# Moving one of eight convolution groups from the middle of a fused kernel to behind its last table

## The chip, the core and the metric

The kernel runs on one core of a Trainium2 chip. The metric is the device time of one execution in microseconds (us); the median of three runs is given. The core has five engines, each with its own instruction queue: TensorE (PE, matrix products, with its weight loads listed as PEld), VectorE (DVE), ScalarE (ACT), GpSimd (POOL) and SyncE (SP, which mostly issues DMA transfers). They wait for each other through semaphores. PE writes to PSUM, and DVE or ACT must carry the result from there to SBUF ("evacuation").

## What is computed

Two long convolutions over 2048 steps and 448 channels share one input x, and a gate mixes them. Branch A builds its convolution kernel K from a table of complex powers; branch B multiplies a shifted k with v first and has its kernel given as data (`ssm_k`).

```python
g = sigmoid((x * gate_w).sum(-1))
# A: state space convolution, K[d, l] = Re sum_n C dB exp(dt A l)
P = exp(logdA[:, :, None] * l)            # the power table, 448 x 256 x 2048
K = einsum("dn,dnl,dn->dl", Cc, P, dB).real
a = causal_conv(u=x, K) + x * Dskip
# B: gated convolution
kv = shift_conv4(k, shift_k) * v
b = x * (causal_conv(kv, ssm_k) + kv * ssm_D)
return g * a + (1 - g) * b                # bf16, 1 x 2048 x 448
```

The reference does both causal convolutions by FFT. The kernel does them with matrix products: a two-stage transform of the signal and of the convolution kernel, a product, and a two-stage way back.

## The kernel before

The channels are cut into four groups of 4 x 28 (`NC = 28`), for each branch: groups ("A", 0..3) and ("B", 0..3). The convolution kernels of A are made by eight table blocks, `block(0)` to `block(7)`, two for each A group. A block is a run of DVE multiplications and additions (the power table in factors TQ and TP), 224 small matmuls that sum over the modes into `pk`, an evacuation of the sums, a gather, and a spread:

```python
def block(self, j, evac, behind=None):      # KGen
    ...                                     # DVE: TQ and TP, in one chain of order
    self.last = chain[0]                    # the last DVE operation of this table
    with self.tc.high_priority(offset=100000):
        ...                                 # PE: 14 x 2 x 2 x 4 matmuls into pk
        self.summed = evac(S[:], pt.rearrange("p n b -> p b n"))   # ACT
    return S
```

A convolution group goes through these helpers. `evac` is a copy on ACT.

```python
def spread_in(cols):                        # first half of the transform: 56 matmuls, 4 evacuations
    zs = qt([P, 32, 4 * NC], "zs")
    spread(nc, psum, Wc, zs, cols, ...)
    return zs

def transform(nc, psum, W, zs, evac, ...):  # second half: 32 matmuls, 4 evacuations
    ...

def swapped(zs, op=None):                   # a copy with its halves exchanged, by two DMAs
    swap = qt([P, 32, 4 * NC], "zsS")
    for r in range(2):
        d = nc.sync.dma_start(swap[64 * r:64 * r + 64], zs[64 - 64 * r:128 - 64 * r])
        ...                                 # behind op, the evacuation of a table's sums
    return zs, swap

def products(nc, X, S, Y, k0=0, k1=32):     # two DVE multiplications of 128 x 3584
    fl = lambda t: t[:, k0:k1].rearrange("p k c -> p (k c)")
    for t in (S, X):
        nc.vector.tensor_tensor(out=fl(t), in0=fl(t), in1=fl(Y), op=ALU.mult)
    return X, S

def stage_a(nc, psum, pool, R, terms, evac):      # way back, first stage: 56 matmuls, 4 evacuations to U
    ...
def stage_b(nc, psum, G, U, consume, banks=2):    # second stage: 128 matmuls, consume per half
    ...
def epilogue_B(H):                                # ug = conv * ug on DVE, from PSUM, twice a group
    ...
```

The loop over the groups consumes one group (`c`), prepares the next (`n`), and builds one table in each step:

```python
def step(c, n, j):
    kind, H = n
    if kind == "B":
        KB[H] = spread_in(skc.pop(H))
        XB[H] = spread_in(kv_cols(H))
    else:
        XA[H] = spread_in(u_cols(H))
    with tc.high_priority(offset=300000):
        U = stage_a(nc, psum, qp, R, terms[c], evac)
    if kind == "B":
        transform(nc, psum, W2, KB[H], evac)
        transform(nc, psum, W2, XB[H], evac)
    else:
        transform(nc, psum, W2, XA[H], evac)
    with tc.high_priority(offset=200000):
        stage_b(nc, psum, G, U, (hold_y if c == ("A", NQG - 2) else epilogue_A if c[0] == "A" else epilogue_B)(c[1]))
    ...
    block(j)
    if kind == "B":
        with tc.high_priority(offset=200000):
            terms[n] = products(nc, *swapped(KB[H], kg.summed), XB[H])
    else:
        XA[H] = swapped(XA[H], kg.summed)
    if kind == "A" and H < NQG - 1:
        transform(nc, psum, W2, KA[H], evac)
        with tc.high_priority(offset=200000):
            terms[n] = products(nc, *XA[H], KA[H])

seq = [("B", 0), ("B", 1), ("B", 2), ("A", 0), ("B", 3), ("A", 1), ("A", 2), ("A", 3)]
for j in range(NBLK - 1):
    step(seq[j], seq[j + 1], j)

# the tail: the last table and the last A group, in two halves
U = qt([P, 2, 64, NC], "U")
...
transform_half(nc, psum, W2, KA[3], evac, 0)
last(0)                                     # products of the first half
block(NBLK - 1)                             # the last table
transform_half(nc, psum, W2, KA[3], evac_two, 1)
stage_a_half(nc, psum, U, R, XA[3], evac, 0)
last(1)
mix_y(NQG - 2)
stage_a_half(nc, psum, U, R, XA[3], evac, 1)
stage_b(nc, psum, G, U, epilogue_A(3), 1)   # stores the output as it goes
```

The large tiles (`zs`, `zsS`, `zsK`, `U`, and the two pairs of `kv` blocks) share a pool of 8 buffers (`NBQ`); PSUM work shares 3 buffers. The order of instructions on each engine isn't that of the program text: a scheduler builds it from the dependencies, the priorities (`high_priority` with a larger offset goes first) and a time model, when the kernel is built.

Of the kernel before, what the change touches and what calls it, by code (L numbers as in the profile page):

```python
# [10 lines left out]
ALU = mybir.AluOpType  # L11
# [6 lines left out]
P = 128  # L18
# [4 lines left out]
NQG = 4  # L23
NC = 112 // NQG
CB = NC // 2
NBLK = 2 * NQG
# [25 lines left out]
def after(tc, ins, before):  # L52
    tc.add_manual_dep(ins.ins, before.ins.name,
                      mybir.DependencyInfo(mybir.DependencyClass.NoSync, mybir.DependencyReason.DATA),
                      reason="order on one engine")
# [6 lines left out]
class Consts:  # L62
# [67 lines left out]
    def stage_a(self, s_col, off_col):  # L130
        nc = self.nc
        j = self.iota("sa_j", [[1024, 64]])
        ph = self.carve(256).rearrange("p (i b) -> p i b", i=4)
        for i, off in enumerate((off_col[0][:, 0:1], off_col[1][:, 0:1], HALF, QUARTER)):
            self.phases(ph[:, i, :], j, s_col, off)
        R = self.pool.tile([P, 256], bf16, name="sa_R")
        nc.scalar.activation(R[:], low16(ph.rearrange("p i b -> p (i b)")), ACT.Sin, scale=PHASE)
        return R

    def stage_b(self, pool, qt, hqt, k_col, mask):  # L140
        nc = self.nc
        G = pool.tile([P, 64, 2, 4, 32], bf16, name="sb_G")
        jv = self.iota("sb_j", [[8, 16], [512, 32]]).rearrange("p (b a) -> p b a", b=16)
        offs = self.pool.tile([P, 4, 2], f32, name="sb_offs")
        for b0 in range(0, 64, 16):
            ph = qt([P, 16, 2, 32], "sb_ph", i32)
            for r, turn in enumerate((QUARTER, HALF)):
                o = offs[:, b0 // 16, r:r + 1]
                nc.vector.tensor_scalar(out=o, in0=k_col[:], scalar1=8.0 * b0, scalar2=turn, op0=ALU.mult, op1=ALU.add)
                self.phases(ph[:, :, r, :], jv, k_col, o)  # L150
            v = pool.tile([P, 16, 2, 32], bf16, name="sb_v", tag="kg_P4", bufs=2)
            nc.scalar.activation(v[:].rearrange("p b r a -> p (b r a)"), low16(ph[:].rearrange("p b r a -> p (b r a)")),
                                 ACT.Sin, scale=PHASE)
            for g in range(4):
                nc.vector.tensor_scalar(out=G[:, b0:b0 + 16, :, g, :], in0=v[:], scalar1=mask[:, g:g + 1], scalar2=None, op0=ALU.mult)
        return G
# [64 lines left out]
def transform(nc, psum, W, zs, evac, ks=range(4)):  # L221
    n = 4 * NC
    for kk in ks:
        pt = psum.tile([P, 2, 512], f32, name="ps_2", tag="ps")
        for i in range(8):
            k = 8 * kk + i
            nc.tensor.matmul(pt[:, i // 4, (i % 4) * n:(i % 4 + 1) * n], lhsT=W[:, k].rearrange("p r s -> p (r s)"), rhs=zs[:, k],  # L227
                             start=True, stop=True)
        evac(zs[:, 8 * kk:8 * kk + 8].rearrange("p (i k) c -> p i (k c)", i=2), pt[:, :, 0:4 * n], kk % 2)
# [6 lines left out]
def transform_half(nc, psum, W, zs, evac, half):  # L236
    for kk in range(2):
        pt = psum.tile([P, 2, 512], f32, name="ps_2", tag="ps")
        for i in range(16):
            k = 16 * kk + i  # L240
            nc.tensor.matmul(pt[:, i // 8, (i % 8) * 56:(i % 8 + 1) * 56], lhsT=W[:, k].rearrange("p r s -> p (r s)"),
                             rhs=half_of(zs, k, k + 1, half), start=True, stop=True)
        for i in range(2):
            k0 = 16 * kk + 8 * i
            evac(half_of(zs, k0, k0 + 8, half), pt[:, i, 0:448].rearrange("p (k c) -> p k c", c=CB), i)


def stage_a_half(nc, psum, U, R, terms, evac, half):
    for j in range(half * CB, half * CB + CB, 7):
        pt = psum.tile([P, 8, 128], f32, name="ps_a", tag="ps")  # L250
        for i in range(7):
            for n, t in enumerate(terms):
                nc.tensor.matmul(pt[:, i, :], lhsT=t[:].rearrange("p k (g c) -> p (k g) c", g=4)[:, :, j + i],  # L253
                                 rhs=R[:, 128 * n:128 * n + 128], start=(n == 0), stop=(n == 1))
        evac(U[:, :, :, j:j + 7].rearrange("p r b c -> p (r b) c"), pt[:, 0:7].rearrange("p i rb -> p rb i"))

# [23 lines left out]
        consume(b0, n, pt[:, :, 0:448])  # L280


def products(nc, X, S, Y, k0=0, k1=32):
    fl = lambda t: t[:, k0:k1].rearrange("p k c -> p (k c)")
    for t in (S, X):
        nc.vector.tensor_tensor(out=fl(t), in0=fl(t), in1=fl(Y), op=ALU.mult)  # L286
    return X, S


# [236 lines left out]
def body(  # L526
# [20 lines left out]
    nc = tc.nc  # L547
# [9 lines left out]
    qp = ctx.enter_context(tc.tile_pool(name="qp", bufs=NBQ))  # L557
    psum = ctx.enter_context(tc.tile_pool(name="psum", bufs=3, space=PSUM))
# [17 lines left out]
    def qt(shape, name, dtype=bf16):  # L576
        return qp.tile(shape, dtype, name=name, tag="q")
# [17 lines left out]
    def spread_in(cols):  # L595
        zs = qt([P, 32, 4 * NC], "zs")
        spread(nc, psum, Wc, zs, cols, [list(range(j, min(j + 8, NC))) for j in range(0, NC, 8)], evac)
        return zs

    def swapped(zs, op=None):  # L600
# [3 lines that stand above are left out]
            if op is not None:  # L604
                behind_other(tc, d, op)
        return zs, swap
# [40 lines left out]
    for b0 in range(56, -1, -8):  # L647
        pt = psum.tile([P, 2, 512], f32, name="ps_v", tag="ps")
        t = qt([P, 4, 8, 112], "kvt")
        for n, tau in enumerate((3, 2, 1, 0)):  # L650
            V.tensor_tensor(out=t[:, n], in0=kt[:, b0 + 3 - tau:b0 + 11 - tau, :],  # L651
                            in1=wt[:, tau, :].unsqueeze(1).to_broadcast([P, 8, 112]), op=ALU.mult)
# [9 lines left out]
    W2 = cons.stage_2(cons.field("b2", 0, 63), [cons.field("o2%d" % r, 6, 1, -QUARTER, (1 + r) * QUARTER) for r in range(2)], kgp, wtc)  # L662
    k_col, mask_b = cons.field("kB", 2, 31, 4.0, 1.0, pool=wp), cons.onehot("mgB", 4, cons.field("gB", 0, 3), 1.0 / 2048, pool=wp)
    R = cons.stage_a(cons.field("sA", 0, 63), [cons.field("oA%d" % r, 6, 1, HALF, (1 - r) * QUARTER) for r in range(2)])
    tb = Tables(tc, kgp, qt, hqt, psum, raw, ident, dt, xfd, nc.sync)
    tb.coefficients()
    G = cons.stage_b(kgp, qt, hqt, k_col, mask_b)
    KB = [None] * NQG
    XB = [None] * NQG
# [36 lines left out]
    kg = KGen(tc, kgp, pk, psk, cons, sel_d, d4, ET)  # L706
# [3 lines left out]
    def block(j):  # L710
        H = j // 2
        if j and j % 2 == 0:
            tb.chunk(H, kg.mid)
        if KA[H] is None:
            KA[H] = qt([P, 32, 4 * NC], "zsK")
        S = kg.block(j, evac, kvl if j == 0 else None)
        with tc.high_priority(offset=100):
            KT = kg.gather(j, S, evac)
            at = (j % 2) * CB
            cols = lambda c: KT[:, :, c]  # L720
            if j >= NBLK - 2:
                spread(nc, psum, WcK, KA[H], cols, [range(0, 7), range(7, 14)], evac, at=at)
            else:
                spread(nc, psk, WcK, KA[H], cols, [range(0, 4), range(4, 8), range(8, 11), range(11, 14)], evac, 4, "ps_g", at)
# [40 lines left out]
    def kv_cols(H):  # L765
        return lambda c: kvq[H][:, :, c]

    def u_cols(H):
        return lambda c: uu[:, :, H * NC + c]

    def step(c, n, j):
        kind, H = n
        if kind == "B":
            KB[H] = spread_in(skc.pop(H))
            XB[H] = spread_in(kv_cols(H))
        else:
            XA[H] = spread_in(u_cols(H))
        with tc.high_priority(offset=300000):
            U = stage_a(nc, psum, qp, R, terms[c], evac)
        if kind == "B":  # L780
            transform(nc, psum, W2, KB[H], evac)
            transform(nc, psum, W2, XB[H], evac)
        else:
            transform(nc, psum, W2, XA[H], evac)
        with tc.high_priority(offset=200000):
            stage_b(nc, psum, G, U, (hold_y if c == ("A", NQG - 2) else epilogue_A if c[0] == "A" else epilogue_B)(c[1]))
        if kind == "B" and H + 1 < NQG:
            skc[H + 1] = sk_cols(H + 1)
        block(j)
        if kind == "B":  # L790
            with tc.high_priority(offset=200000):
                terms[n] = products(nc, *swapped(KB[H], kg.summed), XB[H])
        else:
            XA[H] = swapped(XA[H], kg.summed)
        if kind == "A" and H < NQG - 1:
            transform(nc, psum, W2, KA[H], evac)
            with tc.high_priority(offset=200000):
                terms[n] = products(nc, *XA[H], KA[H])

    terms, skc = {}, {1: sk_cols(1)}  # L800
# [15 lines left out]
    pairs = lambda t: t[:].rearrange("p b (n t) -> p b n t", t=2)  # L816
    V.tensor_tensor(out=pairs(ug), in0=pairs(uu), in1=og[:].unsqueeze(2).to_broadcast([P, 64, 56, 2]), op=ALU.mult)

    seq = [("B", 0), ("B", 1), ("B", 2), ("A", 0), ("B", 3), ("A", 1), ("A", 2), ("A", 3)]
    for j in range(NBLK - 1):  # L820
        step(seq[j], seq[j + 1], j)

    U = qt([P, 2, 64, NC], "U")

    def last(half):
        for k0 in (0, 16):
# [3 lines left out]
    transform_half(nc, psum, W2, KA[3], evac, 0)  # L830
    last(0)
    block(NBLK - 1)
    transform_half(nc, psum, W2, KA[3], evac_two, 1)
    stage_a_half(nc, psum, U, R, XA[3], evac, 0)
    last(1)
# [38 lines left out]
```

## Time and profile before

| | before |
|---|---|
| time, median of 3 | 326.08 us (326.0 to 326.8) |
| span of the profiled run | 323.5 us |
| busy: PE, PEld | 225.5 us (70%), 197.4 us (61%) |
| busy: DVE, ACT | 277.2 us (86%), 243.2 us (75%) |
| busy: POOL | 34.6 us (11%) |
| mean granted TensorE clock | 0.800 |

The profile is one execution. Busy time counts the instructions of an engine. A digit in the busy strips is the busy share of one of 40 equal slices, in tenths; PEclk is the granted clock of TensorE in tenths of full speed. In a timeline a bracket such as `[1.10 <-PE ps_b L279]` says that the engine was idle for 1.10 us before this instruction and what ended the wait; L279 is a line of the kernel. `zs<-ps_c 128x1024 bf16<-128x1024 f32` says which tile is written from which, and the shapes and types.

### The profile page before, as it was taken

The page shows a single profiled execution, that of the slowest core. Times are in us where ns is not written, and L with a number is a line of the kernel's source. Part 1 is how long each engine was busy: PE and PEld are TensorE (multiplying, and loading weights), DVE is VectorE, ACT ScalarE, POOL GpSimd, SP SyncE. Part 2 cuts the span into 40 slices and gives each one's busy share as a digit, 9 for nine tenths or more (in the row PEclk, how much of TensorE's full clock was granted, in tenths as well). Part 3 has the DMA queues.
Part 4 walks back from the last instruction along what each step waited for, and adds up shares of the span by engine and source line. Part 5 has one row for each costly group of instructions (what it writes and reads, how often), then busy time and mean ns, then how long its engine had stood idle before and what let it go on. Part 6 is the DMA issues. An engine that isn't in the chain of part 4 may idle for free.

```text
span 323.5 us, 11944 instructions
## 1 busy us (share of the span) xinstructions
PE 225.5 (70%) x5286; PEld 197.4 (61%) x5286; DVE 277.2 (86%) x571; ACT 243.2 (75%) x395; POOL 34.6 (11%) x129
## 2 busy tenths in 40 slices
PE   0498617737278678699997857999774779966740
PEld 0144607237167568588886846998674678865740
DVE  7999999967999899979999998988999889942450
ACT  3655888779991799998989999689989474936600
POOL 9400002912000009000000000000000000000000
PEclk9999855796758767967997975899998559995765
DMA  6889999730000530050040015004000500040048
GB/s 129 137 188 152 165 164 168 239 59 0 2 0 4 117 57 3 5 158 2 4 102 19 4 45 116 3 4 97 22 2 4 115 3 4 12 108 2 2 91 140
DMA packets 53740, 21.41 MB, mean 66 GB/s; under 512 B 49080, under 2 KB 52024, under 8 KB 53688
## 3 DMA queue, kind: packets, MB, share of 16 engines
q1 hardware_dynamic: 48936, 19.47, 31.6%
q10 hardware_dynamic: 4560, 1.15, 2.0%
q8 instruction: 41, 0.67, 0.9%
q14 instruction: 11, 0.09, 0.1%
q0 software_dynamic: 192, 0.03, 0.1%
HBM read 10.09 MB, written 3.21 MB: 41 GB/s over the span
## 4 chain that ended last, share of the span: by engine, by line
ACT 39%; PE 26%; SPq 14%; DVE 9%; POOL 4%; issue 3%; DMA 3%; ACTq 0%; DVEq 0%; POOLq 0%
ACT zs L565 12%; PE ps_b L279 7%; PE pk L371 6%; ACT ET L481 6%; ACT U L565 5%; ACT zsK L565 5%; PE ps_c L215 5%; SPq L634 4%; POOL skraw L592 4%; PE ps L227 3%; SPq L587 3%; PE ps_a L265 3%; ACT ET L493 3%; SPq L631 2%; ACT ET L511 2%
## 5 line engine op out<-in xcount | busy, mean ns | idle before, releaser
L565 ACT CAST zs<-ps_c 128x1024 bf16<-128x1024 f32 (+1 forms) x48 | 42.5, 940 | 4.8 <-PE ps_c L215 4.7
L227 PEld LDWEIGHTS <-s_W 128*128 128x128 bf16 x480 | 34.4, 118 | 16.7 <-issue 14.2
L318 DVE TENSOR_TENSOR kg_P<-kg_TQ,ET 128x896 bf16<-128x896 bf16 (+1 forms) x64 | 43.8, 705 | 0.3
L565 ACT CAST zs<-ps 128x896 bf16<-128x896 f32 x48 | 41.4, 929 | 1.6 <-PE ps L227 1.5
L227 PE MATMUL ps<-zs,s_W 128*128 128x112 bf16 x384 | 32.2, 252 | 12.2 <-ACT zs L565 6.3
L371 PE MATMUL pk<-kg_TP,kg_TQ 128*21 128x32 bf16 x1792 | 30.3, 238 | 8.5 <-issue 6.3
L371 PEld LDWEIGHTS <-kg_TQ 128*21 128x21 bf16 x1792 | 27.8, 121 | 10.3 <-issue 9.6
L265 PE MATMUL ps_a<-sa_R,zs 128*128 128x128 bf16 x196 | 29.0, 240 | 6.8 <-ACT U L565 4.5
L592 POOL TENSOR_TENSOR skraw<-skraw,dB 128x28 bf16<-128x28 bf16 x4 | 23.3, 5816 | 94.9 <-DMA skraw<-in_B_ssm_k_dram 94.9
L565 ACT CAST U<-ps_a 128x1024 bf16<-128x1024 f32 (+2 forms) x32 | 29.3, 947 | 3.5 <-PE ps_a L253 1.8
L318 DVE TENSOR_TENSOR kg_P<-kg_TP,ET 128x1792 bf16<-128x1792 bf16 (+1 forms) x32 | 30.8, 963 | 0.0
L279 PEld LDWEIGHTS <-sb_G 128*128 128x128 bf16 x1024 | 27.9, 99 | 3.9 <-issue 3.6
L279 PE MATMUL ps_b<-U,sb_G 128*128 128x28 bf16 x1024 | 28.1, 179 | 2.9 <-ACT U L565 1.3
L265 PEld LDWEIGHTS <-zsS 128*128 128x128 bf16 x196 | 26.2, 153 | 5.2 <-issue 5.2
L265 PE MATMUL ps_a<-sa_R,zsS 128*128 128x128 bf16 x196 | 28.5, 239 | 0.0
L265 PEld LDWEIGHTS <-zs 128*128 128x128 bf16 x196 | 26.2, 152 | 2.6 <-DVE zs L286 1.7
L323 DVE TENSOR_TENSOR kg_TQ<-kg_P 128x896 bf16<-128x896 bf16 (+2 forms) x64 | 27.7, 442 | 0.2
L493 ACT ACTIVATE ET<-ks_ph 128x448 bf16<-128x448 int16 x40 | 23.8, 603 | 5.0 <-DVE ks_ph L489 4.0
L565 ACT CAST zsK<-ps_c 128x512 bf16<-128x512 f32 (+2 forms) x28 | 22.1, 798 | 7.0 <-PE ps_c L215 6.9
L215 PE MATMUL ps_c<-WcK,kg_KT 128*64 128x128 bf16 x224 | 19.9, 305 | 9.1 <-ACT zsK L565 5.8
L655 PE MATMUL ps_v<-kvt,scratch 128*128 128x448 bf16 x64 | 16.3, 387 | 13.5 <-DVE kvt L651 13.1
L215 PE MATMUL ps_c<-Wc,kv 128*64 128x128 bf16 x224 | 15.6, 321 | 14.1 <-DVE kv L680 7.8
(141 smaller groups left out, 481.4 us busy)
## 6 DMA issues: line engine op xcount, KB each, us to landing
zsS<-zs SPq DMA_DIRECT2D x16, 448.0 KB, 5.6
kt<-in_B_k_dram SPq DMA_DIRECT2D x16, 112.0 KB, 4.3
skraw<-in_B_ssm_k_dram SPq DMA_DIRECT2D x16, 112.0 KB, 3.6
vt<-in_B_v_dram SPq DMA_DIRECT2D x4, 448.0 KB, 6.8
uu<-in_A_u_dram SPq DMA_DIRECT2D x4, 448.0 KB, 8.7
xfd<-ks_hold SPq DMA_DIRECT2D x2, 672.0 KB, 6.9
ks_xf<-xfd SPq DMA_DIRECT2D x3, 336.0 KB, 3.0
out_dram<-ug SPq DMA_DIRECT2D x8, 112.0 KB, 4.8
```

The lines of the kernel that those rows point to most:

```text
L215: nc.tensor.matmul(pt[64 * r:64 * r + 64, i, :], lhsT=x, rhs=W[:, 128 * r:128 * r + 128], start=True, stop=True, tile_position=(0, 64 * r))
L227: nc.tensor.matmul(pt[:, i // 4, (i % 4) * n:(i % 4 + 1) * n], lhsT=W[:, k].rearrange("p r s -> p (r s)"), rhs=zs[:, k], start=True, stop= ...
L265: nc.tensor.matmul(pt[:, i, :], lhsT=t[:].rearrange("p k (g c) -> p (k g) c", g=4)[:, :, j + i], rhs=R[:, 128 * n:128 * n + 128], start=(n ...
L279: nc.tensor.matmul(o, lhsT=G[:, b, r].rearrange("p g a -> p (g a)"), rhs=U[:, r, b], start=(r == 0), stop=(r == 1))
L318: put(V.tensor_tensor(out=P4[:, i:i + m].rearrange("p n v c m -> p n v (c m)"), in0=in0, in1=in1, op=ALU.mult))
L323: put(V.tensor_tensor(out=T[:, dst:dst + v.shape[1] // 2].rearrange("p n v m -> p (n v) m"), in0=v[:, :, 0], in1=v[:, :, 1], op=ALU.add))
L371: nc.tensor.matmul(pt[32 * g:32 * g + NQ, hw, :].rearrange("p (i j) -> p i j", i=2), lhsT=TQ[:, :, c, m], rhs=rhs, start=(hf == 0 and c == 0),
L481: ex = nc.scalar.activation(dst, x, ACT.Exp, scale=float(e))
L493: sn = nc.scalar.activation(dst.rearrange("p b c m -> p b (c m)"), low16(ph[:].rearrange("p b c m -> p (b c m)")).rearrange("p (b x) -> p ...
L565: return nc.scalar.copy(dst, src)
L592: nc.gpsimd.tensor_tensor(out=raw[:, :, 0], in0=raw[:, :, 0], in1=dB[:, H * NC:(H + 1) * NC], op=ALU.add)
L655: nc.tensor.matmul(pt[:, i, 0:448], lhsT=ident, rhs=t[:, n, 4 * i:4 * i + 4, :].rearrange("p b l -> p (b l)"), start=(n == 0), stop=(n == 3))
```

## The change

Group ("B", 3) leaves its place in the middle. In the loop its slot becomes `None`: step 3 (the fourth, as steps and tables are counted from 0) then prepares nothing and step 4 consumes nothing, while both still build their tables. Its spreads and transforms are done in step 6 (the seventh), beside those of ("A", 3), and the exchange of halves behind the sums of table 6. Its two products are ordered on DVE behind the last operation of the last table, and its two stages of the way back with their epilogue come after `block(7)`, ahead of the second half of ("A", 3). The tile U of ("A", 3) is taken after them. The purpose is to take work out of the stretch in which DVE builds tables, and to do it while the engines wait in the tail. The work itself stays the same: the same instructions of the same shapes.

```diff
--- before.py
+++ after.py
@@ -280,10 +280,12 @@
         consume(b0, n, pt[:, :, 0:448])
 
 
-def products(nc, X, S, Y, k0=0, k1=32):
+def products(nc, X, S, Y, behind=None, k0=0, k1=32):
     fl = lambda t: t[:, k0:k1].rearrange("p k c -> p (k c)")
     for t in (S, X):
-        nc.vector.tensor_tensor(out=fl(t), in0=fl(t), in1=fl(Y), op=ALU.mult)
+        op = nc.vector.tensor_tensor(out=fl(t), in0=fl(t), in1=fl(Y), op=ALU.mult)
+        if behind is not None:
+            behind(op)
     return X, S
 
 
@@ -768,29 +770,42 @@
     def u_cols(H):
         return lambda c: uu[:, :, H * NC + c]
 
+    def consume_a(c):
+        with tc.high_priority(offset=300000):
+            return stage_a(nc, psum, qp, R, terms[c], evac)
+
+    def consume_b(c, U):
+        with tc.high_priority(offset=200000):
+            stage_b(nc, psum, G, U, (hold_y if c == ("A", NQG - 2) else epilogue_A if c[0] == "A" else epilogue_B)(c[1]))
+
     def step(c, n, j):
-        kind, H = n
+        kind, H = n if n else (None, None)
         if kind == "B":
             KB[H] = spread_in(skc.pop(H))
             XB[H] = spread_in(kv_cols(H))
-        else:
+        elif kind == "A":
             XA[H] = spread_in(u_cols(H))
-        with tc.high_priority(offset=300000):
-            U = stage_a(nc, psum, qp, R, terms[c], evac)
+        if c:
+            U = consume_a(c)
         if kind == "B":
             transform(nc, psum, W2, KB[H], evac)
             transform(nc, psum, W2, XB[H], evac)
-        else:
+        elif kind == "A":
             transform(nc, psum, W2, XA[H], evac)
-        with tc.high_priority(offset=200000):
-            stage_b(nc, psum, G, U, (hold_y if c == ("A", NQG - 2) else epilogue_A if c[0] == "A" else epilogue_B)(c[1]))
+        if j == NBLK - 2:
+            KB[3] = spread_in(skc.pop(3))
+            XB[3] = spread_in(kv_cols(3))
+            transform(nc, psum, W2, KB[3], evac)
+            transform(nc, psum, W2, XB[3], evac)
+        if c:
+            consume_b(c, U)
         if kind == "B" and H + 1 < NQG:
             skc[H + 1] = sk_cols(H + 1)
         block(j)
         if kind == "B":
             with tc.high_priority(offset=200000):
                 terms[n] = products(nc, *swapped(KB[H], kg.summed), XB[H])
-        else:
+        elif kind == "A":
             XA[H] = swapped(XA[H], kg.summed)
         if kind == "A" and H < NQG - 1:
             transform(nc, psum, W2, KA[H], evac)
@@ -816,11 +831,11 @@
     pairs = lambda t: t[:].rearrange("p b (n t) -> p b n t", t=2)
     V.tensor_tensor(out=pairs(ug), in0=pairs(uu), in1=og[:].unsqueeze(2).to_broadcast([P, 64, 56, 2]), op=ALU.mult)
 
-    seq = [("B", 0), ("B", 1), ("B", 2), ("A", 0), ("B", 3), ("A", 1), ("A", 2), ("A", 3)]
+    seq = [("B", 0), ("B", 1), ("B", 2), ("A", 0), None, ("A", 1), ("A", 2), ("A", 3)]
     for j in range(NBLK - 1):
         step(seq[j], seq[j + 1], j)
 
-    U = qt([P, 2, 64, NC], "U")
+    KB[3] = swapped(KB[3], kg.summed)
 
     def last(half):
         for k0 in (0, 16):
@@ -830,6 +845,9 @@
     transform_half(nc, psum, W2, KA[3], evac, 0)
     last(0)
     block(NBLK - 1)
+    terms["B", 3] = products(nc, *KB[3], XB[3], lambda op: after(tc, op, kg.last))
+    consume_b(("B", 3), consume_a(("B", 3)))
+    U = qt([P, 2, 64, NC], "U")
     transform_half(nc, psum, W2, KA[3], evac_two, 1)
     stage_a_half(nc, psum, U, R, XA[3], evac, 0)
     last(1)
```

## The prediction

> **What bounds the kernel now.** I read the page's busy strip first, because the change moves work from one part of the run to another and a mean over the run can't value that. One digit is a slice of 323.5 / 40 = 8.1 us.
>
> ```profile
> PE   0498617737278678699997857999774779966740
> DVE  7999999967999899979999998988999889942450
> ACT  3655888779991799998989999689989474936600
> PEclk9999855796758767967997975899998559995765
> ```
>
> From slice 14 (113 us) to slice 34 (284 us) VectorE (DVE) is at 9 nearly throughout, ScalarE (ACT) close behind. From slice 35 on all three engines show holes. So there are two regimes, and I asked for the busy time of each engine in stretches. The columns are the stretch, its length, the busy time of PE, weight loads, DVE, ACT and POOL, the granted clock, the DMA share and GB/s.
>
> ```profile
> 158.00:172.00 14.00, 12.27 (x417) 10.97 (x406) 14.00 (x41) 12.54 (x21) 0.00 (x0) 1.00 0.33 71
> 172.00:186.00 14.00, 11.31 (x310) 11.03 (x311) 13.86 (x27) 13.97 (x25) 0.00 (x0) 0.88 0.01 2
> 186.00:200.00 14.00, 8.69 (x183) 7.27 (x173) 14.00 (x27) 14.00 (x33) 0.00 (x0) 0.67 0.29 68
> ...
> 256.00:270.00 14.00, 10.52 (x303) 9.42 (x299) 12.78 (x18) 7.10 (x9) 0.00 (x0) 0.64 0.08 20
> 270.00:284.60 14.60, 14.20 (x334) 13.38 (x334) 14.57 (x27) 12.74 (x17) 0.00 (x0) 1.00 0.12 26
> 284.60:314.00 29.40, 19.22 (x565) 17.84 (x563) 11.82 (x22) 12.58 (x17) 0.00 (x0) 0.71 0.17 37
> ```
>
> The last power table's vector work ends at 284.6 us. Up to there DVE is the bound (14.00 of 14.00, 14.57 of 14.60). From 284.6 to 314 it works 11.8 of 29.4 us, ACT 12.6, PE 19.2: that tail is a chain of latencies, and no engine is full. The last 9.5 us are output transfers, which the change leaves alone. The chain of work that ended last shows what the tail consists of (start, length, what):
>
> ```profile
> 285.00 1.53 PE pk L371 x73
> 286.53 1.38 issue
> 287.90 2.12 PE pk L371 x115
> 290.02 1.33 issue
> 291.36 0.23 PE pk L371 x2
> ```
>
> The table's products go through PE, then come the evacuation of the sums, gather, spread, second transform, products, the two conv stages and the stores, each waiting for the one before.
>
> **What the Trainium skill says.** "Perfetto Trace Analysis", Optimization Strategy, says that where the most contended engine changes over time, interleaving the regimes can help. That is the idea here, and the two regimes are in the trace. "PSUM — Partial Sum Buffer", Engine vs sequencer instructions, says that ScalarE and VectorE queues are strict first-in first-out and that matmuls start and complete in program order. The trace's order fits (no matmul overtakes another in the timeline), and it is why fill work put ahead of a chain's next link delays that link. "VectorE: DVE Perf Modes", Why PSUM operands drop a tier, says an f32 PSUM operand runs at the lowest rate; here the multiply of 128x896 out of PSUM takes 1.09 us against 0.62 us for 128x896 out of SBUF, so it agrees. "TensorE: Matmul & The Clock Gate", What's actually happening, says PE falls to half clock after an idle window of about 3.4 us. The trace shows a mean clock of 0.50 from 292 to 300 us, though the idle times just before it that I see are only 1.3 to 1.4 us.
>
> **The change, part by part.** I call the fourth gated-convolution group B3.
>
> 1. *Taken from the DVE-bound middle.* The two products and two gated epilogues of B3 are these instructions (start, length):
>
> ```profile
> 202.77 2.02 DVE L286 TENSOR_TENSOR zsS<-zsS,zs 128x3584 bf16<-128x3584 bf16 x1
> 204.70 2.02 DVE L286 TENSOR_TENSOR zs<-zs 128x3584 bf16<-128x3584 bf16 x1
> ...
> 221.76 1.09 DVE L732 TENSOR_TENSOR ug<-ps_b,ug 128x896 bf16<-128x896 f32 x1 [1.10 <-PE ps_b L279]
> ...
> 223.97 1.08 DVE L732 TENSOR_TENSOR ug<-ps_b,ug 128x896 bf16<-128x896 f32 x1
> ```
>
> From start to start a product costs 1.94 us and an epilogue 1.01 us: 2 x 1.94 + 2 x 1.01 = 5.9 us. The bracket on the first epilogue is 1.10 us of DVE waiting for B3's last conv stage, which goes too. Together 5.9 + 1.1 = **-7.0 us** for the moment at which the last table is done.
>
> 2. *Moved within the middle.* Spreading and transforming B3's two operands moves from the fourth step (around 160 to 202 us) to the seventh. On ACT that is 8 spread evacuations at 0.94 us and 8 transform evacuations at 0.93 us (the page's group means), 15.0 us, or some 13 us as they follow one another. On PE it is 112 spread matmuls and 64 transform matmuls, the latter 3.15 us for each 32, so some 12 us. It leaves a stretch where ACT was full (13.97 of 14, 14.00 of 14), but DVE was equally full there, so nothing is gained but item 1. It arrives where ACT has 14 - 7.00 = 6.9 us free (256 to 270) and 1.9 us (270 to 284.6), and PE 3.5 and 0.4 us. Before 256 there are 3.1 us free on ACT and 5.1 on PE (242 to 256: 10.91 and 8.87 of 14). ACT's holes come to 11.9 us against 13, and PE's to 9.0 against 12; B3's own two conv stages leave a further 3.6 us on ACT and 7 us on PE, but earlier, around 208 to 224. So it nearly fits if the order lets it start early, since its inputs were loaded long before. Some of it is likely to push the seventh table's sums, or to end after the eighth and last table and bring B3 late into the tail. I put **+1.5 us**, a judgement.
>
> 3. *Added to the tail.* After the last table: products 3.9 us on DVE; stage A on PE, 56 matmuls that followed one another at 63 ns at full clock (3.5 us) and at 107 ns at half clock (6.0 us); 4 evacuations of U on ACT, some 3.5 us; stage B on PE, 128 matmuls, 3.4 us; 2 epilogues of 1.0 us. DVE waits 6.8 us in the tail before its first half of the last products and 5.5 us later, so its 5.9 us fit in holes. ACT stands 5.3 us waiting for the sums, where U's evacuations fit. PE is the tight one: 6.9 us more in 29.4 - 19.2 = 10.2 us of idle time, of which 2.7 are the issue gaps within the table's sums, 1.3 the wait for U and some 3 the last epilogues' time. That leaves about 3.5 us to fill, so about 6.9 - 3.5 = **+3.4 us**. Stage A and B also carry a higher scheduling priority than the sums, so they may stand ahead of them on PE.
>
> Sum: 326.1 - 7.0 + 1.5 + 3.4 = **324.0 us**.
>
> **The rivals.**
> - *The tail swallows everything.* For it: every engine has holes there, and PE's half clock (0.50 from 292 to 300) might rise with more work: stage A of the last group had 22 matmuls 107 ns apart, which at 63 would give 1.0 us back. Against it: PE is in order and the chain needs PE between nearly all its links. Then 326.1 - 7.0 + 0.5 = 319.6 us.
> - *Given back in the tail.* All 6.9 us of PE work stand ahead of the sums or of the gather. For it: the priorities, and PE's order. Then 326.1 - 7.0 + 6.9 = 326.0 us, no change that matters.
> - *Late preparation.* PE works 14.20 of 14.60 us from 270 to 284.6 at full clock already. If B3's 12 us of PE work go there, the seventh table's sums, or the second step of the last convolution, move back; and B3's half swap (5.6 us from issue to landing in the page) starts after the last table. Then the tail gets 4 to 6 us more: 328 to 331 us. Against it: about 9 us of holes on PE and 12 on ACT from 242 on.
> - *Buffers.* The second pair of kv blocks and B3's tiles live until the seventh step, where up to 8 or 9 tiles want 8 buffers. A wait there would show as a late spread or swap and joins the case above.
>
> **Range and chances.** The gain side is measured (7.0 us off DVE); the two costs are judged, 0.5 to 6.9 for the tail and 0 to 6 for the preparation. The best case gives some 319, the worst some 332, and the generated order of all instructions changes with the diff, which I allow a few us either way. I take 318.5 to 330.5. Faster by over 2% means below 319.6, which needs nearly the best case: 0.20. Slower by over 2% means above 332.6, which needs late preparation and a full tail: 0.07.
>
> **What would show each step.** Step 1: DVE's last table ends near 278 to 279 us instead of 284.6. Step 2: the spreads of ssm_k and kv of B3 show between 235 and 270 us, and ACT and PE are near full to the end of the last table; wrong if DVE gets new waits before it, or if those spreads come after it. Step 3: from the last table's end to the last epilogue 32 to 33 us instead of 29, with B3's products in the former 6.8 us hole and the sums on PE ending later. The prediction is wrong below 318 if the tail doesn't grow at all or the middle loses more than the 7.0 us, and above 331 if the B3 products wait for their swap after the last table.

## The result and the profile after

The changed kernel takes 342.69 us against 326.42 us for the kernel before on the same chip: a ratio of 1.0497, with a 95% interval of 1.0462 to 1.0532. It is 16.3 us slower.

The page's busy strips of the changed kernel show where. A slice is now 8.5 us.

```profile
PE   0598325845497587799827887939759949847740
DVE  7899999977997999799999999999999930171640
ACT  2745978599954899979768597889846837874320
PEclk9999965678587679589958759678969997996995
```

DVE's run of nines ends with slice 32, at 272 us, so the tables are done sooner than before. What follows is no longer 29 us of tail but 56, and in its first half PE and ACT do most of the work while DVE nearly stands still. The stretches (columns as before the change) say the same in numbers:

```profile
172.00:186.00 14.00, 7.81 (x161) 7.22 (x160) 13.93 (x28) 9.71 (x19) 0.00 (x0) 0.65 0.01 1
186.00:200.00 14.00, 11.16 (x377) 10.31 (x369) 13.29 (x25) 10.18 (x27) 0.00 (x0) 0.71 0.11 28
...
270.00:284.00 14.00, 8.69 (x350) 7.93 (x348) 4.83 (x7) 7.42 (x11) 0.00 (x0) 0.88 0.30 69
284.00:298.00 14.00, 12.46 (x277) 11.40 (x273) 1.93 (x4) 12.41 (x16) 0.00 (x0) 1.00 0.29 68
```

From 172 to 200 us ACT, which had been full (27.97 of 28 us), has 8.1 us free. Most of the work taken out there comes back from 284 to 298, where ACT is busy for 12.41 of 14 us. On the timeline of DVE the last table operation, the held output of (A, 2), B3's products and B3's epilogues now stand here:

```profile
273.77 1.09 DVE L330 TENSOR_TENSOR kg_TP<-kg_TP,ET 128x1792 bf16<-128x1792 bf16 x1
295.73 0.62 DVE L764 TENSOR_TENSOR y<-y,gb 128x896 bf16<-128x896 bf16 x1 [20.87 <-ACT y L567]
...
303.19 2.02 DVE L286 TENSOR_TENSOR zsS<-zsS,zs 128x3584 bf16<-128x3584 bf16 x1
...
315.51 1.09 DVE L734 TENSOR_TENSOR ug<-ps_b,ug 128x896 bf16<-128x896 f32 x1 [8.37 <-PE ps_b L279]
```

The last table ends at 274.9 us. DVE then waits 20.9 us for ACT, and B3's products start 28 us after that end. The chain that ended last, over the stretch in which the kernel before went from the sums straight to gather and spread, reads (start, length, what):

```profile
274.91 3.10 PE pk L373 x155
278.01 2.86 issue
280.88 0.63 PE pk L373 x26
281.50 2.38 PE ps_c L215 x39
...
287.92 4.98 ACT zs L567 x6
...
307.20 4.94 PE ps_a L265 x48
...
313.71 3.38 PE ps_b L279 x128
```

The `ps_c` matmuls and the `zs` evacuations between 281 and 293 us are B3's preparation. ACT's timeline shows what that does to the last table, from the evacuation of its sums (`kg_S`) to the first one of its gather (`kg_KT`), first of the kernel before, then of the changed kernel:

```profile
291.63 0.53 ACT L565 CAST kg_S<-pk 128x448 bf16<-128x448 f32 x1 [5.31 <-PE pk L371]
...
294.25 0.58 ACT L565 CAST kg_KT<-ps_g 128x448 bf16<-128x448 f32 x1
```

```profile
281.54 0.53 ACT L567 CAST kg_S<-pk 128x448 bf16<-128x448 f32 x1 [6.11 <-PE pk L373]
...
287.92 6.59 ACT L567 CAST zs<-ps 128x896 bf16<-128x896 f32 x8
...
299.18 0.56 ACT L567 CAST kg_KT<-ps_g 128x448 bf16<-128x448 f32 x1
```

That took 2.6 us before and takes 17.6 us now. `ps_a` L265 and `ps_b` L279 from 307 to 317 us are B3's own two stages, so both moved parts lie on the path.

### The profile page after: what moved, and what is told of

Same layout as the page of the kernel before. It is cut to its first block, busy times and chain, and to the rows that moved or that the text cites. A ratio compares the mean times of both kernels' runs of the same rounds, so it can differ in the third digit from the quotient of the medians.

```text
span 340.1 us, 11947 instructions
## 1 busy us (share of the span) xinstructions
PE 228.9 (67%) x5286; PEld 199.4 (59%) x5286; DVE 277.0 (81%) x571; ACT 243.6 (72%) x395; POOL 32.4 (10%) x129
## 4 chain that ended last, share of the span: by engine, by line
DVE 40%; ACT 28%; PE 12%; SPq 6%; DMA 4%; issue 3%; POOL 3%; DVEq 0%; ACTq 0%
DVE kg_P L320 10%; ACT zs L567 9%; ACT ET L483 5%; PE ps_b L279 4%; ACT U L567 4%; DVE zs L286 3%; DVE zsS L286 3%; DVE kg_TQ L325 3%; DVE kg_TP L330 3%; DVE ks_ph L491 3%; DVE kg_TP L325 3%; POOL skraw L594 3%; ACT ks_mag L483 2%; PE pk L373 2%; PE ps_a L265 2%
## 5 line engine op out<-in xcount | busy, mean ns | idle before, releaser
L567 ACT CAST zs<-ps_c 128x1024 bf16<-128x1024 f32 (+1 forms) x48 | 41.6, 923 | 5.6 <-PE ps_c L215 5.6
L265 PE MATMUL ps_a<-sa_R,zs 128*128 128x128 bf16 x196 | 33.2, 263 | 12.1 <-DVE zs L286 7.8
L227 PE MATMUL ps<-zs,s_W 128*128 128x112 bf16 x384 | 30.2, 242 | 11.7 <-ACT U L567 6.0
L265 PEld LDWEIGHTS <-zs 128*128 128x128 bf16 x196 | 28.2, 156 | 8.8 <-DVE zs L286 8.3
L265 PE MATMUL ps_a<-sa_R,zsS 128*128 128x128 bf16 x196 | 32.7, 261 | 0.0
L279 PE MATMUL ps_b<-U,sb_G 128*128 128x28 bf16 x1024 | 27.6, 177 | 5.5 <-ACT U L567 3.7
L279 PEld LDWEIGHTS <-sb_G 128*128 128x128 bf16 x1024 | 27.5, 98 | 6.4 <-issue 6.2
L215 PE MATMUL ps_c<-WcK,kg_KT 128*64 128x128 bf16 x224 | 19.1, 298 | 17.7 <-ACT zsK L567 13.0
L265 PEld LDWEIGHTS <-zsS 128*128 128x128 bf16 x196 | 28.2, 157 | 4.4 <-issue 4.3
L594 POOL TENSOR_TENSOR skraw<-skraw,dB 128x28 bf16<-128x28 bf16 x4 | 21.1, 5277 | 97.8 <-DMA skraw<-in_B_ssm_k_dram 71.1
L215 PEld LDWEIGHTS <-kg_KT 128*64 128x64 bf16 x224 | 16.6, 209 | 20.2 <-issue 14.8
L567 ACT CAST zsK<-ps_c 128x512 bf16<-128x512 f32 (+2 forms) x28 | 21.4, 773 | 6.3 <-PE ps_c L215 6.2
```

What stands on the lines that cost most here:

```text
L215: nc.tensor.matmul(pt[64 * r:64 * r + 64, i, :], lhsT=x, rhs=W[:, 128 * r:128 * r + 128], start=True, stop=True, tile_position=(0, 64 * r))
L279: nc.tensor.matmul(o, lhsT=G[:, b, r].rearrange("p g a -> p (g a)"), rhs=U[:, r, b], start=(r == 0), stop=(r == 1))
L567: return nc.scalar.copy(dst, src)
L594: nc.gpsimd.tensor_tensor(out=raw[:, :, 0], in0=raw[:, :, 0], in1=dB[:, H * NC:(H + 1) * NC], op=ALU.add)
```

## The experiments

Times are medians of 4 executions (run 9: 20, run 11: 6). The points of each tail are read from the timelines of DVE, ACT and PE of one execution (us; "last spread" is the end of the evacuation of the last table's spread, "last half" the start of the second transform half of (A, 3), which needs it):

| kernel | time | last table ends | last spread | last half | last epilogue ends |
|---|---|---|---|---|---|
| before | 326.4 | 284.6 | 299.7 | 299.7 | 313.6 |
| changed | 342.7 | 274.9 | 305.6 | 316.9 | 330.5 |
| 1: no B3 | 317.6 | 275.6 | 292.1 | 292.1 | 306.0 |
| 2: prepared in step 3 | 339.5 | 279.7 | 298.0 | 314.1 | 327.8 |
| 3: prepared in step 4 | 344.6 | 285.3 | 307.5 | 321.0 | 334.5 |
| 4: priority | 342.9 | 276.6 | 308.0 | 318.9 | 332.4 |
| 5: stages behind | 339.7 | 275.2 | 306.8 | 306.9 | 328.6 |
| 6: prepared, exchanged in step 3 | 330.6 | 278.5 | 297.5 | 304.9 | 318.3 |
| 7: as 6, stages ahead of gather | 333.8 | 278.8 | 308.0 | 308.1 | 321.8 |
| 8: late preparation alone | 332.1 | 275.7 | 306.7 | 306.7 | 320.7 |
| 9: early preparation alone | 324.9 | 279.7 | 298.7 | 298.7 | 312.3 |
| 10: as 6, stages behind | 330.8 | 280.0 | 298.8 | 298.9 | 320.5 |
| 11: before, B3 without DVE work | 328.5 | 285.1 | 303.2 | 303.3 | 317.1 |

**1. No B3.** Edit to the changed kernel:

```diff
-        if j == NBLK - 2:
-            KB[3] = spread_in(skc.pop(3))
-            ...
-    KB[3] = swapped(KB[3], kg.summed)
-    terms["B", 3] = products(...)
-    consume_b(("B", 3), consume_a(("B", 3)))
```

> The changed kernel with all work of group (B, 3) left out (its preparation, its products and its two last stages), so its part of the output is missing: the floor of both stretches. Theory (late preparation, held by the order of the PSUM buffers): the last table ends near 275 us as in the changed kernel, the stretch from there to the last epilogue falls back to about 29 us, and the time is 316 to 318 us. Rival (the rearranged step order itself makes the tail long, whatever B3 does): that stretch stays above 40 us and the time above 328 us.

Measured: 317.56 us, ratio 0.975 (0.9728 to 0.9771). The tail is 30.4 us. The new order of the steps does not make the tail long: without B3 it is short. Against the kernel before, leaving out all of B3 brings 325.54 - 317.56 = 8.0 us. A move that keeps B3's work can hardly bring more, except for what a newly built order of instructions changes.

**2. Preparation back in step 3.** `if j == NBLK - 2:` becomes `if j == 3:` in the changed kernel.

> The changed kernel with B3's spreads and transforms back in step 3, where they were before the change; its swap, products and last stages stay behind the last table. Theory: only the place of the preparation made the tail long, so the last table ends at 276 to 279 us, the tail is 32 to 36 us and the time 320 to 325 us. Rival (B3's products and stages at the end are themselves the cost, since PE is in order): the tail stays over 45 us and the time over 333 us.

Measured: 339.47 us, ratio 1.0411 (1.0378 to 1.0444), tail 48.1 us. By the numbers the rival won, but the trace gives another reason than a full PE. The waits of DVE from 285 to 305 us (us in total, times, longest):

```profile
DVE y L764 <- ACT y L567: 9.5, 2, 9.3
DVE zsS L843 <- DMA zsS<-zs: 3.2, 1, 3.2
DVE zsS L286 <- DMA zsS<-zs: 2.9, 1, 2.9
```

B3's operands were ready long before, yet its exchange of halves was issued only from 288.8 us on, and B3's products wait for it until 299.1. In this build the exchange stands in SyncE's queue behind that of (A, 3), and it also waits for a semaphore of PE: its tile takes the buffer of a tile of (A, 2), which stage A of (A, 2) reads. The queue came last. The last of those matmuls ended at 279.4 us, but the exchange of (A, 3) waits for the last evacuation of its transform, which ACT ended at 287.5 us, and was issued then. So the order of SyncE's queue held B3 back, not the lack of a buffer.

**3. Preparation in step 4.** As run 2, with `if j == 4:`.

> The changed kernel with B3's spreads and transforms in step 4, which consumes no group and where ACT has holes. Theory: as with step 3, perhaps 1 to 2 us better because ACT is less full: 319 to 324 us, tail 32 to 36 us. Rival (the end is the cost): over 333 us.

Measured: 344.59 us, ratio 1.0515 (1.0471 to 1.0559). My theory missed here in two ways. The time is over the rival's 333 us, and the tables now end at 285.3 us, so the whole gain of the middle is gone, though ACT had holes in step 4 and DVE had lost 5.9 us of work. From 100 us to the end of the last table DVE waits 15.7 us here against 6.2 in the changed kernel, 5.9 of them for ACT's sines. In the tail B3's products again wait for their exchange, until 307.6 us, as in run 2: that of (A, 3), ahead of it in SyncE's queue, was issued only at 296.1 us, when its transform was done.

**4. Preparation late, at the highest priority.** The four lines in step 6 stand under `with tc.high_priority(offset=300000):`.

> The changed kernel with the preparation still written in step 6 but at the highest scheduling priority (300000). Theory (tiles of the shared PSUM pool are handed out in the order of the program text, so priority can't move the preparation ahead of what is written before it): it starts after the second transform of (A, 3) as before, near 271 us, and the time stays at 338 to 346 us. Rival (it came late only because its priority was low): it starts before 255 us and the time falls to 320 to 328 us.

Measured: 342.86 us, ratio 1.0526 (1.0498 to 1.0554). The theory held. ACT's timeline of this run has the last evacuation of the transform of (A, 3), then at once B3's first spread, and the last table's sums behind all but two of B3's evacuations:

```profile
274.86 0.99 ACT L567 CAST zs<-ps 128x896 bf16<-128x896 f32 x1
275.65 2.03 ACT L567 CAST zs<-ps_c 128x1024 bf16<-128x1024 f32 x2
...
291.00 0.54 ACT L567 CAST kg_S<-pk 128x448 bf16<-128x448 f32 x1
```

The priority moved B3 ahead of the sums, which come later in the text on another PSUM pool, but not ahead of anything written before it on the shared one. In the built programs of the kernel before, the changed kernel and all these runs, PE starts the tiles of the shared PSUM pool (up to 177 of them) in the order of the program text without one exception. Three buffers are handed round in that order.

**5. Stages behind.** In the changed kernel:

```diff
     terms["B", 3] = products(...)
-    consume_b(("B", 3), consume_a(("B", 3)))
 ...
     stage_a_half(nc, psum, U, R, XA[3], evac, 1)
+    consume_b(("B", 3), consume_a(("B", 3)))
```

> The changed kernel with B3's two last stages written behind the stage A halves of (A, 3) instead of ahead of its second transform half; the preparation stays late in step 6. Theory (the second half of (A, 3) waits in PSUM order behind B3's stages, which wait for B3's products): that transform half starts as soon as its spread is evacuated, near 306 us instead of 317, though B3's stages then follow it; in all 3 to 6 us less, 336 to 340 us. Rival (the late preparation alone is the cost): 341 to 344 us.

Measured: 339.74 us, ratio 1.044 (1.0411 to 1.047). PE's timeline, first of the changed kernel, then of this run, has the last spread and the last half:

```profile
302.38 1.87 PE L215 MATMUL ps_c<-WcK,kg_KT 128*64 128x128 bf16 x28 [1.46 <-ACT kg_KT L567]
313.71 3.36 PE L279 MATMUL ps_b<-U,sb_G 128*128 128x28 bf16 x128 [1.08 <-ACT U L567]
316.93 0.99 PE L241 MATMUL ps<-zsK,s_W 128*128 128x56 bf16 x32
```

```profile
303.58 1.92 PE L215 MATMUL ps_c<-WcK,kg_KT 128*64 128x128 bf16 x28 [1.46 <-ACT kg_KT L567]
306.89 1.65 PE L241 MATMUL ps<-zsK,s_W 128*128 128x56 bf16 x32 [1.40 <-ACT zsK L567]
```

The wait of 11.3 us between spread and last half is gone, as the PSUM order says; B3's stages then push the last stage B instead, and of the 11.3 us only 2 to 3 are gained (1.9 us by the ratios, 3.0 by the medians).

**6. Preparation and exchange in step 3.** As run 2, with `KB[3] = swapped(KB[3], kg.summed)` after `block(3)` instead of after the loop.

> Preparation in step 3 as in the earlier run, and now the exchange of halves too; only B3's products and two stages stay behind the last table. Theory (with the preparation early, what held B3 back was its exchange, waiting for a free one of the 8 buffers until the stages of (A, 2) were done): the products start within 1 us of the last table's end, the tail falls from 48 to 34 to 38 us, the time is 323 to 329 us. Rival (B3's work at the end is the cost whatever it waits for): tail over 43 us and over 333 us.

Measured: 330.63 us, ratio 1.0175 (1.0133 to 1.0216). The products now follow the last table at once:

```profile
277.44 1.09 DVE L330 TENSOR_TENSOR kg_TP<-kg_TP,ET 128x1792 bf16<-128x1792 bf16 x1
278.45 2.02 DVE L286 TENSOR_TENSOR zsS<-zsS,zs 128x3584 bf16<-128x3584 bf16 x1
```

The direction is the theory's, 8.8 us off run 2, though the expected reason, a missing buffer, was not what came last there. The tail of 39.8 us is longer than I said and the time lies just above my range: the last spread is done at 297.5 us, and the last half waits behind B3's stages for another 7.4 us, until 304.9.

**7. As run 6, stages ahead of the gather.** The products and stages of B3 are written between the sums of the last table and its gather.

> As the run with preparation and exchange in step 3, with B3's products and stages written ahead of the gather and spread of the last table, so their PSUM tiles come ahead of that spread's. Theory (PSUM order): B3's stage A starts some 4 us after the last table's end instead of 13 or more, in the time in which PE and ACT wait for the sums, the tail is 31 to 35 us and the time 319 to 324 us, below the kernel before. Rival (PE is simply full in the tail, order doesn't matter): the same time as the other run within 1 us.

Measured: 333.81 us, ratio 1.0261 (1.0223 to 1.0298). Neither expectation is met. B3's stage A started at 292.5 us, 14 us after the last table, not 4, since the transform of (A, 3), the last stage of (A, 2), the first spread and the first half of (A, 3) are still ahead of it in the shared order. It then delayed the gather:

```profile
300.35 0.59 ACT L567 CAST U<-ps_a 128x512 bf16<-128x512 f32 x1 [2.03 <-PE ps_a L265]
301.34 0.54 ACT L567 CAST kg_KT<-ps_g 128x448 bf16<-128x448 f32 x1 [0.40 <-PE ps_g L414]
```

The tail wasn't waiting for work at its beginning: PE and ACT enter it with the last groups' work unfinished.

**8 and 9. Preparation alone, late and early.** Run 8 is the changed kernel and run 9 is run 6, both without these lines:

```diff
-    terms["B", 3] = products(...)
-    consume_b(("B", 3), consume_a(("B", 3)))
```

> The changed kernel with B3's products and two last stages left out, so its part of the output is missing; the preparation and the exchange stay in step 6. Theory (two costs that add up: the preparation ahead of the last table's spread, some 16 us, and B3's stages ahead of the last transform half, some 11 us): the last transform half starts near 306 us, when its spread is evacuated, and the time is 329 to 333 us. Rival (only one chain: without B3's products and stages the late preparation fits in holes): under 322 us.

> Preparation and exchange in step 3, B3's products and two last stages left out, so its part of the output is missing. Theory (of the 13 us between the run without B3 and the run with early preparation, 7 are B3's stages ahead of the last transform half, the rest the preparation in the middle): 322 to 325 us. Rival (all 13 us come from the stages at the end): 317 to 319 us.

Measured: run 8 332.11 us, ratio 1.0204 (1.0177 to 1.0232); run 9 324.90 us, ratio 0.999 (0.9969 to 1.0012). Both as the theory had it. With runs 1 and 6 and the changed kernel they make a table of B3's two parts (us):

| | no preparation | early | late |
|---|---|---|---|
| without products and stages | 317.6 | 324.9 | 332.1 |
| with them behind the last table | | 330.6 | 342.7 |

The preparation costs 7.3 us early and 14.5 late; the rest costs 5.7 and 10.6 more.

**10. As run 6, stages behind.** Run 6 with the edit of run 5.

> Preparation and exchange in step 3, and B3's two last stages written behind the stage A halves of (A, 3). Theory: the last transform half no longer waits (7 us less), but B3's stages then stand ahead of the last stage B and give most of it back: 326 to 330 us, no better than the kernel before. Rival (they fit in the holes of the last group's stages): 322 to 325 us, better than the kernel before.

Measured: 330.84 us, ratio 1.016 (1.0121 to 1.0199), just above the theory's range. The last half starts at once (298.9 us), and B3's stages ahead of the last stage B take all of it back.

**11. The kernel before, B3 without vector work.** In the kernel before, `products` of ("B", 3) is left out, and its epilogue returns without its multiplication:

```diff
+                if H == 3:
+                    terms[n] = swapped(KB[H], kg.summed)
...
+            if H == 3:
+                return
```

> The kernel before with only B3's vector work left out: its two products and two epilogues (5.9 us of DVE and no other engine's work; the output of B3 is wrong by what is left out). The preparation and both last stages stay in the middle. Theory now (the tables on DVE and the evacuations on ACT, chained through the PSUM order, end together, so shortening DVE alone leaves the end where the PE and ACT work of the last groups puts it): the last table ends 4 to 7 us earlier, but the tail grows by most of that, and the time is 323 to 325.5 us. Rival (step 1 of the prediction: DVE is the bound up to the last table, so its 5.9 us are gained in full): 319 to 320.5 us.

Measured: 328.50 us, ratio 1.0079 (1.0055 to 1.0103): DVE has 5.9 us less work, and the kernel is 0.8% slower. Neither expectation is met: the last table doesn't even end earlier (285.1 against 284.6 us). DVE's waits up to 285 us, first of the kernel before, then of this run:

```profile
DVE ET L506 <- ACT ET L493: 2.3, 2, 1.5
```

```profile
DVE ET L506 <- ACT ET L493: 8.9, 5, 4.4
```

The time taken from DVE came back as waiting; the wait for ACT's sines in the table's entries alone grew by 6.6 us. The instruction order is built anew for each program, so a part of this may be its order and not the work left out; the two aren't told apart here.

No version beat the kernel before with B3's work complete.

## Why the prediction was wrong

The prediction was 324.0 us with a range of 318.5 to 330.5; measured were 342.7. The sum's three terms, against runs 1, 8 and the changed kernel:

| step | predicted | measured |
|---|---|---|
| last table ends earlier | -7.0 | -9.7 |
| time, B3 taken out of the middle | -7.0 | -8.0 (run 1) |
| preparation in step 6 | +1.5 | +14.5 (run 8 less run 1) |
| products and stages behind the last table | +3.4 | +10.6 (changed less run 8) |

The kernel before, run again beside each set of runs, took 325.5 to 326.4 us, so the terms add to 17.1 where 16.3 were measured.

**Step 1, the bound.** The work taken from DVE was sized rightly, but not what the end gains by it. From 100 us to the end of the last table, DVE's busy time and its waits for other engines are (us):

| kernel | DVE busy | DVE waits | last table ends |
|---|---|---|---|
| before | 174.3 | 10.1 | 284.6 |
| changed | 168.1 | 6.2 | 274.9 |
| 1: no B3 | 168.6 | 6.4 | 275.6 |
| 9: early preparation alone | 168.3 | 11.0 | 279.7 |
| 11: before, B3 without DVE work | 168.5 | 16.0 | 285.1 |

The work falls by some 6 us in each, as predicted. The waits are what differs: they fell by 3.9 us where I had put 1.1, and in runs 9 and 11 they rise. I took DVE's 14.00 of 14.00 us as proof that its work is what the end waits for. Runs 9 and 11 speak against that, though both have a newly built order. In run 9 the preparation is early and B3's products and stages are missing altogether, and the time is that of the kernel before: the last table ends 4.9 us sooner, but the tail is longer by 3.6. In run 11 only DVE work is missing and nothing is gained. By runs 1 and 9, B3's early preparation accounts for 7.3 of the 8.0 us, and it has no DVE work in it. So the nearness of -7.0 to -8.0 is luck. That ACT and the shared PSUM order are level with DVE in the middle is my reading; no run shows it by itself.

**Step 2, the step that failed.** I wrote that the preparation "nearly fits if the order lets it start early, since its inputs were loaded long before", added up ACT's and PE's holes and judged +1.5; it cost 14.5 us. The condition was the mistake. The order doesn't let it: its PSUM tiles come after the transform of (A, 3) in the text, that after stage A of (A, 2), and that waits for products done at 261.8 us. So the first spread of B3 ran at 271.6 us, 3 us before the last table's end, and holes before 256 us were of no use. Run 4 shows that priority can't repair it. In the tail 12 us of B3's evacuations, from 282.5 to 294.5 us, stand on ACT in front of the last table's gather, and the last spread is done 30.7 us after the last table instead of 15.1. The rival "late preparation" had this place right, with 4 to 6 us for it and 328 to 331 us in all. But it argued from a full PE and not from the order of the buffers, and its size was too low. The sign that I had named for a time above 331 us, B3's exchange after the last table, came true: it was issued at 291.3 us. (In the sum of ACT's holes, 14 - 7.00 should read 14 - 7.10; its result of 6.9 us is right.)

**Step 3, the tail.** Adding PE's idle time and subtracting was the wrong sum again: a hole counts only if the fill work is ready in it and nothing behind it needs the buffer. (The idle times listed there leave 3.2 us to fill and not 3.5, which matters little.) B3's exchange had landed by 297.1 us, but its products stand on DVE behind the first products of (A, 3) and began at 303.2 us, 28 us after the last table. The early holes had passed, and B3's stages stood between the last spread and the last half, 11.3 us (run 5 removes that wait). Even with preparation and exchange early, the wait is 7.4 us and the cost 5.7 us (run 6, and run 6 less run 9). That is nearer to the 6.9 us of the rival "given back in the tail" than to my 3.4. Most of the 3.5 us of holes that I had credited were not there to be used.

**The buffers.** In the changed kernel they did no visible harm: B3's exchange goes when its operand is ready. In run 2 the exchange came late by the order of the queue and not by a buffer.

**Free capacity and order.** In the Trainium skill, "Perfetto Trace Analysis" (Optimization Strategy) says that interleaving regimes may improve performance. Here it did not, with 10.2 us of PE's time idle in the tail of the kernel before: that regime is a chain in a fixed order, not free capacity. "PSUM — Partial Sum Buffer" (Engine vs sequencer instructions) says that the queues of ScalarE, VectorE and GpSimd are strictly first-in first-out. The changed kernel's trace agrees for VectorE: B3's products, ready by 297.1 us, started only behind those of (A, 3), at 303.2 us. I had quoted this page and not applied it to where B3's work stands.

## What to carry to other kernels

Before moving work into idle time, write down the order in which shared buffers, PSUM above all, are handed out, and place the work in that order: its start is set by what stands before it, and all that stands behind it waits. An engine that is busy all the time isn't yet what the end waits for; check whether the next one is just as full, or leave the work out once and see what its waits and the end do. If preparation, exchange and use move together, each must be ready for the next at the new place, or the move only makes the last chain longer.

## What was not expected of the hardware

- Within the 224 matmuls that sum a table PE stands still without any wait that the profile shows: 1.38 and 1.33 us in the last table of the kernel before, 2.86 us in that of the changed kernel. Both are on the chain that ended last. In the last table of the other runs the gaps come to 3.7, 3.2 and 3.5 us in runs 5, 8 and 11, to 0.8 to 1.0 us in runs 1, 2, 3, 6, 7, 9 and 10, and to nothing in run 4. So some 2.4 us of the 14.5 that the late preparation costs (3.2 in run 8 less 0.8 in run 1) may stand in them, but run 4 is as slow without them. What causes the gaps isn't settled.
- The granted clock of PE was higher over the changed tail: 0.91, with PE busy for 39.2 of 55.6 us, against 0.71 over the tail before, with 19.2 of 29.4. The tail was longer all the same.
